# Moving one transposition and two product groups in the first block of a TensorE-bound kernel

## The chip, the cores and the metric

The kernel runs on one core of a Trainium2 chip. The metric is device time in microseconds (us) of that core; lower is better. Before the change the median of the first three runs was 1027.58 us. All runs compared here are of the fast state. The granted clock is the share of its full clock at which TensorE was allowed to run; where it differs between runs, the text says so, because that turned out to be the point.

## The reference

Retention (attention with a decay in place of a softmax) for 8 batches of 8 heads and 576 positions, then a two-layer block on 4608 tokens.

```python
scores = scale * q @ k.T                       # 8 x 8 heads, 576 x 576, head size 64
ret = scores * gamma ** (i - j)  (i >= j)      # masked decay
x = (ret @ v) laid out as (4608, 512)
h = x @ w_in                                   # 512 -> 2048
g = h * erf(softplus(h))
out = g @ w_out                                # 2048 -> 512
```

## The kernel before

Tokens come in 36 pieces of 128. Each piece has three stages: `transposes` (queries and keys through TensorE, copied by ScalarE out of PSUM, where this kernel has TensorE write its results), `scores` (TensorE, then a mask on VectorE) and `outputs` (TensorE, then scaling on VectorE; it also carries a state on to the next piece). Four pieces make one chunk of the two-layer block. The stages of later pieces are threaded between the products of earlier chunks, to keep TensorE at work (99% of the span). On ScalarE the trace shows the order in which the program is written: group 13's copy starts at 52.33, behind two rounding operations written ahead of it (51.17 and 51.75).

The first chunk's products come in sixteen groups, four for each quarter of the inner dimension; groups of a quarter need the rounded weights of that quarter. Each of the last four groups ends with a copy on ScalarE. Softplus and erf each begin with a table load on ScalarE (1.28 us each in this trace).

```python
def plain(self):                               # one yield = one group
    ...
    for dc in range(n_dc):                     # four quarters
        for n in range(4):
            for j in range(GP):
                nc.tensor.matmul(acc[n][...], lhsT=wa[...dc...], rhs=t[:, dc, ...])
            if dc == n_dc - 1:
                nc.scalar.copy(out=(self.t2 if tok else self.t1)[:, f], in_=acc[n])
            yield

def transposes(i):
    ...                                        # TensorE into PSUM, then on ScalarE:
    nc.scalar.copy(out=tT, in_=pt)

def rounding():                                # five steps for each part of the weights
    nc.scalar.activation(a_f, high_f, AF.Abs); nc.scalar.mul(...)   # step 1, ScalarE
    ...                                        # steps 2 to 5, VectorE (later parts end on GpSimd)
```

The order of the start is a string: `a` is the next stage of the next piece, `p` the next group, `w` a load of weights, a digit so many steps of rounding, `s` the store of the first chunk's input. Behind it come the softplus and the erf of the first chunk, the eighth piece's outputs, and the second chunk's groups with the ninth piece's stages.

```python
for what in "alkakakawkakakawaa3awwa2aaa5ppappawwppa5ppapp5wawcppa5ppappaa5s":
    ...
firsts[0].softplus()                           # table load, two activations on ScalarE
firsts[0].erf()                                # table load, two activations on ScalarE
most[0] = before_chunk(3)
attend(after_chunk(1))                         # eighth outputs
store_x(1)
for step, _ in enumerate(firsts[1].plain()):
    if step % 2 == 0:
        attend(min(done[0] + 1, most[0]))      # ninth transposition, ninth scores, ...
    round_weights(int(step > 1))
    ...
```

## Time and profile before

| | before |
|---|---|
| median of six runs, three of them taken with the changed kernel | 1027.55 us |
| span of the profiled run | 1026.0 us |
| TensorE busy | 1017.5 us (99%) |
| TensorE's listed waits, 42 to 66 us | 0.8 us ahead of the eighth outputs, 0.7 us ahead of group 9 |
| ScalarE busy | 390.4 us (38%) |

TensorE is the engine that sets the end (89% of the chain that ended last). A row of the view in order of time reads: start in us, length in us, engine, line of the kernel, operation, tile written and tiles read, shapes, count, and in brackets the idle time ahead of it with what ended it. The prediction shows the rows that matter.

### The profile page before, as it was taken

To read this page: it belongs to the slowest core of one execution; us is meant where nothing else is said; L and a number is where in the kernel's file an instruction comes from. 1 tells how busy PE (TensorE), PEld (TensorE's weight loads), DVE (VectorE), ACT (ScalarE), POOL (GpSimd) and SP (SyncE) were. 2 spreads that over 40 slices of the span, in tenths; PEclk is the share of its full clock that TensorE was granted. 3 is DMA by queue.
4 is the path that set the end of the run, shared out by engine and by line. 5 is a ranking of instruction groups with operands and counts; after the bars stand their busy time and mean duration, and the time that the engine had idled before them with its cause. 6 is when DMAs were issued, how large, how long until landed. Compare 5 with 4: busy or idle time off the path is not lost.

```text
span 1026.0 us, 15946 instructions
## 1 busy us (share of the span) xinstructions
PE 1017.5 (99%) x6346; PEld 876.1 (85%) x6346; DVE 669.1 (65%) x1054; ACT 390.4 (38%) x481; POOL 123.7 (12%) x122
## 2 busy tenths in 40 slices
PE   9999999999999999999999999999999999999998
PEld 8778888888888888888888888888888888888887
DVE  3868777877976656656666666666567655555555
ACT  2254134233234444434343444444433333333332
POOL 2143112122312110010001001000100000000000
PEclk9999999999999999999999999999999999999999
DMA  9999889979984344544444345444333334444333
GB/s 197 191 241 194 224 194 221 251 155 248 242 187 161 120 150 145 168 158 163 156 150 163 123 146 160 167 144 144 144 124 124 123 131 126 131 136 133 124 91 115
DMA packets 146986, 165.76 MB, mean 162 GB/s; under 512 B 97376, under 2 KB 121568, under 8 KB 138848
## 3 DMA queue, kind: packets, MB, share of 16 engines
q1 hardware_dynamic: 145904, 163.96, 56.5%
q8 instruction: 50, 0.82, 0.3%
q10 hardware_dynamic: 1008, 0.79, 0.3%
q14 instruction: 24, 0.20, 0.1%
HBM read 117.52 MB, written 47.19 MB: 161 GB/s over the span
## 4 chain that ended last, share of the span: by engine, by line
PE 89%; DMA 5%; DVE 3%; SPq 3%; issue 1%; POOL 0%; DVEq 0%; POOLq 0%
PE a L600 23%; PE a L492 22%; PE g L600 11%; PE g L492 11%; PE e L600 6%; PE e L492 5%; PE s L343 3%; PE o L361 2%; DMA raw_qs<-in_q_dram 1%; PE p L546 1%; SPq L145 1%; PE o L384 1%; PE o L372 1%; DMA raw_k<-in_k_dram 1%; SPq L131 1%; DMA raw_ks<-in_k_dram 1%
## 5 line engine op out<-in xcount | busy, mean ns | idle before, releaser
L492 PE MATMUL a<-x,wa 128*128 128x256 f32 x1088 | 258.3, 380 | 0.0
L492 PEld LDWEIGHTS a<-x,wa 128*128 128x128 f32 x1088 | 205.7, 190 | 28.5
L600 PE MATMUL a<-wb,s 128*128 128x256 f32 x864 | 205.7, 381 | 0.0
L600 PEld LDWEIGHTS a<-wb,s 128*128 128x128 f32 x864 | 162.9, 190 | 23.6 <-ACT o L614 0.7
L99 DVE TENSOR_TENSOR t<-g,t 128x512 f32<-128x512 f32 x68 | 46.9, 690 | 150.3 <-ACT t L522 113.1
L492 PE MATMUL g<-x,wa 128*128 128x256 f32 x544 | 129.2, 380 | 0.0
L492 PEld LDWEIGHTS g<-x,wa 128*128 128x128 f32 x544 | 102.8, 190 | 14.4
L99 DVE TENSOR_TENSOR o<-a,o 128x512 f32<-128x512 f32 x108 | 74.2, 687 | 49.3 <-PE a L600 49.3
L517 ACT COPY t<-a 128x512 f32<-128x512 f32 x34 | 19.9, 586 | 188.2 <-PE a L492 188.2
L99 DVE TENSOR_TENSOR t<-t,s 128x1024 f32<-128x1024 f32 x72 | 89.6, 1285 | 0.0
L561 ACT ACTIVATE s<-t 128x1024 f32<-128x1024 f32 x72 | 72.1, 1049 | 27.8 <-DVE t L99 27.8
L270 POOL TENSOR_TENSOR wraw<-wraw 128x512 f32<-128x512 f32 x28 | 29.5, 1053 | 435.6 <-DVE wraw L268 178.9
L99 DVE TENSOR_TENSOR x<-x 128x512 f32<-128x512 f32 x115 | 75.8, 692 | 1.2
L528 ACT COPY t<-a 128x512 f32<-128x512 f32 x34 | 19.9, 587 | 144.4 <-PE a L492 144.4
L565 ACT ACTIVATE s<-s 128x1024 f32<-128x1024 f32 x72 | 72.1, 1049 | 0.4
L600 PE MATMUL g<-wb,s 128*128 128x256 f32 x288 | 68.6, 381 | 0.0
L600 PE MATMUL e<-wb,t 128*128 128x256 f32 x288 | 68.5, 380 | 0.0
L600 PE MATMUL a<-wb,t 128*128 128x256 f32 x288 | 68.5, 380 | 0.0
L600 PE MATMUL g<-wb,t 128*128 128x256 f32 x288 | 68.2, 380 | 0.0
L99 DVE TENSOR_TENSOR sT<-s,cst 128x512 f32<-128x512 f32 x72 | 46.2, 682 | 32.5 <-PE s L343 32.5
L99 DVE TENSOR_TENSOR o<-g,o 128x512 f32<-128x512 f32 x72 | 49.3, 684 | 24.6 <-ACT o L614 19.8
L492 PE MATMUL e<-x,wa 128*128 128x256 f32 x272 | 64.8, 381 | 0.0
(75 smaller groups left out, 1226.2 us busy)
## 6 DMA issues: line engine op xcount, KB each, us to landing
od<-o SPq DMA_DIRECT2D x54, 512.0 KB, 3.3
x<-xd SPq DMA_DIRECT2D x27, 1024.0 KB, 4.8
o<-od SPq DMA_DIRECT2D x27, 1024.0 KB, 5.2
raw_qs<-in_q_dram SPq DMA_DIRECT2D x96, 112.0 KB, 4.4
raw_ks<-in_k_dram SPq DMA_DIRECT2D x84, 112.0 KB, 4.1
xd<-x SPq DMA_DIRECT2D x9, 1024.0 KB, 5.3
raw_k<-in_k_dram SPq DMA_DIRECT2D x64, 128.0 KB, 4.5
raw_v<-in_v_dram SPq DMA_DIRECT2D x64, 128.0 KB, 4.5
```

Source lines behind the costliest of these rows:

```text
L99: nc.vector.tensor_tensor(out=out, in0=in0, in1=in1, op=op)
L131: nc.sync.dma_start(out=t[part * SQ : (part + 1) * SQ, :, at : at + m - SQ], in_=tokens[:, :, d0 : d0 + m - SQ])
L145: nc.sync.dma_start(out=t[r0 : r0 + n, e::2, :], in_=heads.rearrange("h p d -> p h d"))
L270: engine.tensor_tensor(out=r_f, in0=high_f, in1=r_f, op=ALU.mult)
L343: nc.tensor.matmul(ps[e][:, p, :], lhsT=t["kT"][heads[e], p, :], rhs=t["qT"][heads[e], p, :], start=True, stop=True)
L361: nc.tensor.matmul(o[p % 2][heads[(e + p) % 2], p // 2, :], lhsT=t["v"][:, 2 * p + e, :], rhs=t["sT"][:, e, p, :], start=(p < 2), stop=(no ...
L492: nc.tensor.matmul(acc[:, j * TH : (j + 1) * TH], lhsT=weights["wa", self.g][:, a, d, j * P : (j + 1) * P], rhs=x[self.g, self.c][a][:, d, :],
L517: nc.scalar.copy(out=self.t1[:, 1], in_=self.a)
L528: nc.scalar.copy(out=self.t2[:, 0], in_=self.a)
L561: nc.scalar.activation(self.s[:, j], t, AF.Softplus)
L565: nc.scalar.activation(self.s[:, j], self.s[:, j], AF.Erf)
L600: nc.tensor.matmul(acc[:, tp, :], lhsT=left[:, j * TH + tp * P : j * TH + (tp + 1) * P], rhs=weights["wb", self.g][:, b, j, :], start=(sta ...
```

## The change

It is meant to fill TensorE's two waits in the first chunk: the seventh piece's transposition (and the load of weights `w` behind it) goes ahead of the third quarter (groups 9 and 10), which waits for its weights, and groups 15 and 16 go behind the eighth scores, so that they run while VectorE masks those scores and the eighth outputs find their mask ready.

```diff
-    for what in "alkakakawkakakawaa3awwa2aaa5ppappawwppa5ppapp5wawcppa5ppappaa5s":
+    for what in "alkakakawkakakawaa3awwa2aaa5ppappawwppa5ppawapp5wcppa5ppaaapp5s":
```

## The prediction

> **What bounds the kernel now.** I read four views in this order: the page, the totals of TensorE's waits, TensorE in order of time from 43 to 65 us, and ScalarE over the same stretch. First the page.
>
> ```profile
> span 1026.0 us, 15946 instructions
> PE 1017.5 (99%) x6346; PEld 876.1 (85%) x6346; DVE 669.1 (65%) x1054; ACT 390.4 (38%) x481; POOL 123.7 (12%) x122
> PEclk9999999999999999999999999999999999999999
> PE 89%; DMA 5%; DVE 3%; SPq 3%; issue 1%; POOL 0%; DVEq 0%; POOLq 0%
> ```
>
> TensorE is busy 1017.5 of 1026.0 us at full clock and carries 89% of the chain that ended last. So only its 8.5 idle us can be saved, while a new TensorE wait lengthens the run by its full size, because almost nothing later can absorb it: after 64 us one wait is listed, of 0.2 us (last line here). The first three lines are the totals of the waits from 42 to 66 us.
>
> ```profile
> PE o L361 <- POOL state L423: 0.8, 1, 0.8
> PE p L546 <- DVE wa L271: 0.7, 1, 0.7
> PEld o L361 <- DVE sT L99: 0.4, 1, 0.4
> ...
> PE s L343 <- DVE kT L322: 0.2, 1, 0.2
> ```
>
> The change aims at these waits. I number pieces and groups from one: group 1 to 16 are the first block's products (L546, two to a row of x8), piece 7's transposition is the first pt_q row below, pt_k with it. TensorE in order of time (start, length):
>
> ```profile
> 44.40 1.99 PE L546 MATMUL p<-x,wa 128*128 128x256 f32 x8 [0.72 <-DVE wa L271]
> 46.23 0.60 PE L328 MATMUL pt_q<-ident,raw_q 128*128 128x128 f32 x4
> ...
> 50.02 1.99 PE L546 MATMUL p<-x,wa 128*128 128x256 f32 x8
> ...
> 52.72 1.03 PE L546 MATMUL pe<-x,wa 128*128 128x256 f32 x4
> 53.59 1.03 PE L546 MATMUL pg<-x,wa 128*128 128x256 f32 x4
> 54.54 1.09 PE L361 MATMUL o<-sT,raw_v 128*64 128x128 f32 x16
> 56.78 1.16 PE L343 MATMUL s<-qT,kT 64*128 64x128 f32 x16
> 58.76 1.64 PE L361 MATMUL o<-sT,raw_v 128*64 128x128 f32 x16 [0.82 <-POOL state L423]
> ```
>
> The third quarter (groups 9 to 12) starts at 44.40 after waiting 0.72 us for its rounded weights. Groups 15 and 16 (pe, pg) run before the seventh outputs and the eighth scores (56.78); those scores are followed straight by the eighth outputs, which need their mask from VectorE first. The wait is put down to GpSimd's state, but only 2 of the 16 products run before 59.31, when the second mask has ended (59.26): scores end at 57.94, outputs could have gone on at once, so about 1.3 us are lost there.
>
> ScalarE, same stretch:
>
> ```profile
> 53.75 0.60 ACT L334 COPY kT<-pt_k 128x512 f32<-128x512 f32 x1
> 54.23 0.61 ACT L555 COPY t<-pe 128x512 f32<-128x512 f32 x1
> 54.70 0.62 ACT L555 COPY t<-pg 128x512 f32<-128x512 f32 x1
> 55.18 0.73 ACT L250 ACTIVATE wb<-wraw 128x512 f32<-128x512 f32 x1
> 55.76 0.72 ACT L251 ACTIVATE wraw<-wraw 128x512 f32<-128x512 uint32 x1
> 56.50 1.28 ACT L561 ACT_TABLE_LOAD   x1
> 57.79 2.00 ACT L561 ACTIVATE s<-t 128x1024 f32<-128x1024 f32 x2
> 59.81 1.28 ACT L565 ACT_TABLE_LOAD   x1
> 61.11 2.01 ACT L565 ACTIVATE s<-s 128x1024 f32<-128x1024 f32 x2
> 63.15 0.59 ACT L334 COPY kT<-pt_k 128x512 f32<-128x512 f32 x1
> ```
>
> This is what I build on: from the copy of group 16 (54.70) to the copy of the ninth piece's keys (63.15) ScalarE has no gap. That copy ends at 63.74, and the ninth scores, which need it, run at 64.77. The chain has about one microsecond of slack.
>
> [...] group 13's copy starts at 52.33, behind two rounding operations (51.17, 51.75), though its products were through about a microsecond earlier. [...] The trace has 1283 ns for each of two loads here, but the softplus starts 0.01 us behind its load[...]. [...] L255 and L259 take 0.79 and 1.15 us beside GpSimd work at 45.15 to 46.96, against 0.43 when alone.
>
> **The change, part by part.** No instruction is added or removed; the order of loads on the queue, of weight roundings and of PSUM buffers stays. Two stretches of TensorE's order move.
>
> Part one, transposition ahead of group 9. It takes 47.10 - 46.23 = 0.87 us and the idle time before group 9 is 0.72 us, so it fills the wait: group 9 would start at about 43.68 + 0.87 = 44.55 instead of 44.40, and groups 9 to 12 and the seventh scores end at about 49.3 instead of 50.02. Its data is there: the piece's last key load is issued at 36.09 and lands 8.0 us later, 44.1, just when those products are due. But group 13 needs the fourth weight part, whose last step on VectorE ends at 49.94; in the kernel before this is hidden to within 0.1 us. It cannot come earlier, and now comes a little later: its two ScalarE steps, done at 42.25 to 43.54 before, are queued behind the two transposition copies (about 44.4 to 45.5), so VectorE's L255 can start at about 46.1 instead of 45.26; it then waits for GpSimd's value weighting (45.73 plus 1.04 gives 46.8) and ends at about 47.05. L259 to L271 follow with 0.45, 0.72, 0.43+0.1, 0.72, 0.69 between starts and ends: 50.2. So group 13 starts at 50.25, 0.2 later than before. Part one earns nothing: -0.7 turns into +0.2.
>
> Part two, groups 15 and 16 behind the eighth scores. From 50.25: groups 13 and 14 and the eighth transposition 2.70 (52.72 - 50.02), seventh outputs 2.24 (56.78 - 54.54), eighth scores 1.10, groups 15 and 16 1.82 plus 0.1: through at about 58.2. Masks of the eighth scores end at about 57.7, hidden beside those groups. The eighth outputs run from 58.2 to 60.4 instead of ending at 61.54: +0.2 - 1.3 = -1.1 us. This is the intended gain.
>
> The price is on ScalarE. Group 16's copy now waits for group 16: later by seventh outputs and eighth scores, 54.54 to 57.88 = 3.34, plus 0.1, plus the 0.2 above = 3.64 us. All behind it is in order and without a gap, so it moves whole: softplus, erf, and the ninth piece's key copy, which ends at 63.74 + 3.64 = 67.38. TensorE, 1.1 us early, reaches the ninth scores at 64.77 - 1.1 = 63.6 and stands until 67.45. Scores move from 64.77 to 67.45, +2.7 us. Everything behind is TensorE-bound; one small gap ahead of the tenth piece's transposition (67.70 to 67.98, from the same rows) should close, -0.2. Net +2.5 us: 1027.6 + 2.5 = 1030.1.
>
> **Rivals.** (a) The gains stand and the ScalarE chain hides: -1.1 us, or -1.9 if the fourth weight part also came early; 1025.7 to 1026.5. For it: ScalarE is busy only 38% overall. Against: its order puts the ninth keys' copy behind the erf, and those 10 lines have no gap. (b) The stall of 3.8 us at the ninth scores also throttles TensorE. [...] No gap after the start in the trace before is long enough to test it. (c) A load becomes late because the transposition triggers the ninth piece's query load. The queue reaches that load at 54.98 only, long after its trigger, and its order is kept; I give it nothing, at most a few tenths through the 44.1 landing, which the slack ahead of group 13 swallows. (d) Later phases absorb the shift: only 0.2 us of listed waits lie behind 64 us, so 1029.9 at the lowest.
>
> **Range and chances.** Centre 1030.1, with 0.2 for the throttling tail and run spread: 1030.2. Three runs before spread by 1.2 us. Errors of the chain sum are about half a microsecond on either side, so 1028.8 to 1032.0. All rivals stay within 0.5% of the time, far from 2%: same 0.98.
>
> **What would show it.** Part one: the wait of 0.72 us for L271 ahead of group 9 gone, and one of near a microsecond ahead of group 13 in its place, again for L271. Part two: eighth outputs without a wait; group 16's copy near 58.3; a TensorE wait of 3.5 to 4 us at the ninth scores, ended by the key copy on ScalarE; busy time of TensorE unchanged, idle time up. Wrong if the ninth scores start before 65 us, if the key copy runs ahead of the erf, or if TensorE waits for a load in 60 to 70 us.

## The result and the profile after

The changed kernel took 1032.68 us (median of 6 runs, 1030.36 to 1033.56) against 1027.55 us (6 runs). The ratio is 1.0048, with a 95% interval of 1.0035 to 1.0060. Ratios here are the mean time of one kernel's fast runs over that of the other's of the same rounds, so not quite the ratio of the medians. The sign and the place of the loss were as predicted; the size was not: 5.1 us where 2.6 were forecast, and above the stated range.

The page of the changed kernel (same parts as in the prediction: span, busy time, chain that ended last):

```profile
span 1030.6 us, 15945 instructions
PE 1018.5 (99%) x6346; PEld 877.0 (85%) x6346; DVE 666.8 (65%) x1054; ACT 390.2 (38%) x481; POOL 122.4 (12%) x122
PE 95%; DVE 1%; ACT 1%; SPq 1%; DMA 1%; issue 0%; POOL 0%; POOLq 0%; ACTq 0%; DVEq 0%
```

TensorE's busy time grew by 1.0 us though it does the same work, and its idle time by 3.6 us. TensorE's waits of the changed kernel from 42 to 75 us (total, count, longest):

```profile
PE s L343 <- ACT kT L334: 3.4, 1, 3.4
PE p L546 <- DVE wa L271: 1.1, 1, 1.1
```

Both waits of before are gone from their places. The one for L271 now stands ahead of group 13 and has grown, as the prediction said, and a new one of 3.4 us is ended by ScalarE's copy of the ninth keys. TensorE in order of time:

```profile
50.68 1.99 PE L546 MATMUL p<-x,wa 128*128 128x256 f32 x8 [1.09 <-DVE wa L271]
...
57.77 1.03 PE L546 MATMUL pg<-x,wa 128*128 128x256 f32 x4
58.73 1.09 PE L361 MATMUL o<-sT,raw_v 128*64 128x128 f32 x16
...
63.24 1.10 PE L546 MATMUL pe<-x,wa 128*128 128x256 f32 x4
67.73 1.60 PE L343 MATMUL s<-qT,kT 64*128 64x128 f32 x16 [3.39 <-ACT kT L334]
69.25 2.07 PE L546 MATMUL pg<-x,wa 128*128 128x256 f32 x4
```

The eighth outputs (58.73) follow group 16 without a wait: that half of the intent works. The ninth scores then stand until 67.73. The last row is the surprise: the same four instructions that took 1.13 us before take 2.07 us. The same two rows in the kernel before:

```profile
64.77 1.16 PE L343 MATMUL s<-qT,kT 64*128 64x128 f32 x16
65.86 1.13 PE L546 MATMUL pg<-x,wa 128*128 128x256 f32 x4
```

ScalarE in order of time shows who held the scores:

```profile
53.68 0.59 ACT L334 COPY kT<-pt_k 128x512 f32<-128x512 f32 x1
57.97 0.58 ACT L555 COPY t<-pe 128x512 f32<-128x512 f32 x1 [3.70 <-PE pe L546]
58.84 0.59 ACT L555 COPY t<-pg 128x512 f32<-128x512 f32 x1 [0.28 <-PE pg L546]
...
65.20 2.00 ACT L565 ACTIVATE s<-s 128x1024 f32<-128x1024 f32 x2
67.11 0.56 ACT L334 COPY kT<-pt_k 128x512 f32<-128x512 f32 x1
```

It stood 3.70 us waiting for group 15, did the softplus and the erf that much later, and copied the ninth keys last. Stretches of the changed kernel, with busy us and number of instructions of TensorE, its weight loads, VectorE, ScalarE and GpSimd, their granted clock of TensorE, and the DMA's share and GB/s:

```profile
66.00:68.00 2.00, 0.27 (x4) 0.27 (x6) 0.00 (x0) 2.00 (x4) 1.26 (x2) 1.00 0.97 406
68.00:70.00 2.00, 2.00 (x18) 1.69 (x17) 0.65 (x2) 0.80 (x2) 0.00 (x0) 0.57 1.21 262
70.00:72.00 2.00, 2.00 (x7) 1.61 (x6) 2.00 (x6) 0.00 (x0) 0.00 (x0) 0.57 1.16 377
```

After the stall the clock was 0.57 in two stretches of 2 us. The trace's clock record has 0.5 for 3.413 us, from 68.3 us on, and 1.0 on both sides. A window, here and below, is a stretch of that length.

The difference of the two spans, 1030.57 - 1025.96 = 4.61 us, adds up from landmarks in the two traces. To the end of the third weight part (44.34 and 44.68): +0.34, ahead of the change. From there to group 13 (5.68 and 6.00): +0.32. To the ninth scores (14.75 and 17.05): +2.30. To the ninth outputs (5.50 and 6.81): +1.31. The same stretch takes 5.19 us where the clock stays full (e1_fill below), so this is 1.6 us of lowered clock, less the 0.3 us gap ahead of the tenth transposition, which closed. From there to the end (955.69 and 956.03): +0.34, of which a wait at a later piece's scores, 0.2 before and 0.6 after, is the most.

### The profile page after: what moved, and what is told of

Read it like the earlier page. It is cut to its first block, busy times and chain, and to the rows that moved or that the text cites. A ratio compares the mean times of both kernels' runs of the same rounds, so it can differ in the third digit from the quotient of the medians.

```text
span 1030.6 us, 15945 instructions
## 1 busy us (share of the span) xinstructions
PE 1018.5 (99%) x6346; PEld 877.0 (85%) x6346; DVE 666.8 (65%) x1054; ACT 390.2 (38%) x481; POOL 122.4 (12%) x122
## 4 chain that ended last, share of the span: by engine, by line
PE 95%; DVE 1%; ACT 1%; SPq 1%; DMA 1%; issue 0%; POOL 0%; POOLq 0%; ACTq 0%; DVEq 0%
PE a L600 24%; PE a L492 23%; PE g L600 12%; PE g L492 12%; PE e L600 6%; PE e L492 6%; PE s L343 3%; PE o L361 3%; PE o L384 2%; PE o L372 1%; PE p L546 1%; PE pg L546 1%; SPq L145 1%; DMA wraw<-in_moe_w_in_dram 1%; PE pe L546 1%; PE idle L706 0%
```

## The experiments

Theory: ScalarE's order moves the ninth keys' copy behind the late softplus and erf, TensorE stalls for it (3.4 us), and the stall brings a window at half clock, as the changed kernel's trace has it (0.5 for 3.413 us). All experiments ran on one chip (that of the first result is not on record), with the kernel before in the same rounds; there its medians were 1028.33, 1028.10 and 1028.53 us, and single runs spread over 3 to 4 us, so ratios and the recorded clock of each run count for more than a median. I call a run lowered when its mean clock is 0.998 or less; all 102 runs of the kernel before in these rounds have 0.999 or 1.000.

**The stall filled (e1_fill).** The changed kernel, with products of no use in the idle stretch, into a PSUM bank that is overwritten next.

```diff
+                    if (self.c, dc, n) == (1, 0, 2):
+                        for _ in range(12):
+                            nc.tensor.matmul(acc[3][:, :P], lhsT=ident, rhs=ident, start=True, stop=True)
```

> The changed kernel with 12 identity products (some 3.2 us of TensorE work of no use) put just ahead of the ninth scores, into the idle stretch. Theory (the stall lets the clock be halved for one window of 3.413 us, worth 1.7 us): the ninth scores still start near 67.7, but the granted clock is 1.0 after it, every run lies near 1030.4, as the one unthrottled run of the changed kernel (1030.36). Rival (the extra 2 us come from something else behind the stall, loads or VectorE): still 1032 to 1033.5.

Measured: 1030.28 us (10 runs), ratio 1.0019 (1.0009 to 1.0028); no run lowered. TensorE in order of time:

```profile
67.42 1.16 PE L343 MATMUL s<-qT,kT 64*128 64x128 f32 x16 [0.69 <-ACT kT L334]
68.52 1.13 PE L546 MATMUL pg<-x,wa 128*128 128x256 f32 x4
```

The scores start as late as in the changed kernel and the next group again takes 1.13 us, at a mean clock of 0.999. Work that does nothing made the kernel faster: the mean is 1030.43 us, against 1032.18 for e3_part_two (below), which has the stall unfilled in the same rounds. So the clock's share of the loss is shown. Two of the ten runs reached 1031.4 and 1032.2 us at full clock; on this chip that is within the spread that the kernel before has too.

**Part one alone (e2_part_one).** The load `w` moves with the transposition, as in the change.

```diff
-    ..."ppa5ppapp5wawcppa5ppappaa5s"
+    ..."ppa5ppawapp5wcppa5ppappaa5s"
```

> Only the transposition ahead of group 9. Theory: the wait of 0.7 us moves to group 13, where the fourth weight part comes 0.2 to 0.4 us later than before; 1027.6 to 1028.0, no stall above 1.5 us, no lowered clock. Rival (the part's gain is real and hidden in the changed kernel by the other): 1026.8.

Measured: 1028.02 us (13 runs), ratio 0.9999 (0.9991 to 1.0007), none lowered. Group 13 waits 1.1 us for L271 and starts 5.99 us after the third weight part (44.50 to 50.49), against 5.68 before. The part moves the wait and earns nothing that these runs can see.

**Part two alone (e3_part_two).**

```diff
-    ..."ppa5ppappaa5s"
+    ..."ppa5ppaaapp5s"
```

> Only groups 15 and 16 behind the eighth scores. Theory: the whole loss is here: ninth scores about 67.3, stall 3.4 to 3.8 us, most runs 1031.5 to 1033 with one window at half clock, a rare one near 1030. Rival (both parts are needed for the loss): within 0.5 us of the kernel before.

Measured: 1032.29 us (5 runs), ratio 1.0039 (1.0026 to 1.0052), all five lowered. The stall is 3.4 us again, and the ninth scores come 22.73 us after the third weight part (44.75 to 67.48), against 20.43 before and 23.05 in the changed kernel: +2.30 of part two and +0.32 of part one make up the whole. The loss is part two's.

**The erf behind the ninth transposition (e4_erf_later).** The changed kernel with one call moved.

```diff
     firsts[0].softplus()
-    firsts[0].erf()
...
             attend(min(done[0] + 1, most[0]))
+        if step == 0:
+            firsts[0].erf()
```

> The changed kernel with the erf emitted after the ninth piece's transposition, so that its key copy is not behind the erf's table load and two activations (3.3 us). Theory (ScalarE's order is the cause): key copy near 64.0, stall at the ninth scores 0.5 to 1.0 us, clock 1.0, 1027.0 to 1027.6, at or a little under the kernel before. Rival (the key copy is late for another reason, or PSUM or VectorE hold the ninth scores): stays above 1029.5.

Measured: 1027.50 us (21 runs), ratio 0.9993 (0.9986 to 0.9999), none lowered. The copy runs at 63.80, before the erf, and the scores follow almost without a gap:

```profile
64.42 1.16 PE L343 MATMUL s<-qT,kT 64*128 64x128 f32 x16
```

One move on ScalarE takes the whole loss away and leaves a gain of about 0.7 us by the ratio (interval 0.1 to 1.4): the cause is the order on ScalarE.

**The changed kernel again (e7_after_again), unaltered.**

> The changed kernel unaltered, to have it on the same chip and in the same rounds as the next three. Theory: stall of 3.4 us at the ninth scores, most runs with a mean clock of 0.996 to 0.998 and 3.5 to 5.5 us over the kernel before; a run with clock 0.999 or 1.000, if there is one, only 1.5 to 3 us over it. Rival (the lowered clock was chance in the first six runs[...]): most runs at 0.999 or 1.000 and about 2.5 us over the kernel before.

Measured: 1032.21 us (5 runs), ratio 1.0038 (1.0024 to 1.0052), all five lowered. The rival of chance falls: with the first six runs and part two alone, 15 of 16 runs with this stall were lowered. Its profile shows a second form of the loss. The clock record has 0.5 for 6.827 us, two windows, from 67.0 us on. TensorE in order of time:

```profile
68.02 2.08 PE L343 MATMUL s<-qT,kT 64*128 64x128 f32 x16 [3.38 <-ACT kT L334]
70.03 2.07 PE L546 MATMUL pg<-x,wa 128*128 128x256 f32 x4
71.89 1.91 PE L546 MATMUL p<-x,wa 128*128 128x256 f32 x4
```

Here the clock was lowered while TensorE still stood, so the scores run slow too. The window from 67.0 to 70.4 had 1.0 us of standing and 2.4 us of work, and the clock was still 0.50 from 70.5 to 73.0; it was 1.00 from 74.0 on.

**Shorter stalls (e8_fill_half, e5_half_erf, e10_fill_nine).** The filled kernel with 6 and with 9 identity products, and the changed kernel with only the second half of the erf moved.

```diff
-                        for _ in range(12):
+                        for _ in range(6):     # e8;  e10: range(9)
```

```diff
-    firsts[0].erf()
+    firsts[0].erf((0,))
...
+        if step == 0:
+            firsts[0].erf((1,))
```

The expectation of e8_fill_half names two outcomes, one after the other: no lowered run at all, or some.

> The filled kernel with 6 identity products in place of 12 (some 1.4 us of work), so about 2.0 us of TensorE stay idle, while the ninth scores start at the same time. [...] never lowered, 2.5 us over the kernel before. [...] lowered in some of the runs (mean clock 0.998 or less), those about 4.5 us over it.

Measured: 1031.48 us (7 runs), ratio 1.0029 (1.0018 to 1.0040). The second outcome came: four of seven lowered (mean clock 0.997 or 0.998); these average 1031.91 us, the other three 1030.68. So a lowered clock cost 1.2 us here, not the 2 us that the expectation gave it. TensorE stood 2.0 us in the profiled run, which kept its full clock.

> The changed kernel with only the second half of the erf (1.0 us) emitted after the ninth piece's transposition. Theory: the key copy is 1.0 us earlier, stall 2.4 us, time without a lowered clock 1.0 us under that of the changed kernel, so some 1.5 us over the kernel before; with 2.4 us idle the clock is lowered in a part of the runs, which then lie 3.2 us over. Rival (ScalarE's order is not what holds the scores): like the changed kernel.

Measured: 1030.59 us (14 runs), ratio 1.0024 (1.0016 to 1.0032). Nine of fourteen lowered, average 1031.33 us, the other five 1029.83. TensorE in order of time:

```profile
67.22 1.16 PE L343 MATMUL s<-qT,kT 64*128 64x128 f32 x16 [2.44 <-ACT kT L334]
```

> The filled kernel with 9 identity products: about 1.3 us of TensorE stay idle at the ninth scores, which start at the same time. From the shares of lowered runs so far (0 of 10 with 0.7 us idle, 4 of 7 with 2.0, 9 of 14 with 2.4, 15 of 16 with 3.4) [...] no run here is lowered (mean clock 0.999 or 1.000 in all), 2 to 2.5 us over the kernel before. If the chance just grows with the idle time: about a third of the runs lowered.

Measured: 1030.58 us (8 runs), ratio 1.0024 (1.0013 to 1.0034). None lowered, with a stall of 1.4 us. So with stalls of 2.0 and 2.4 us, shorter than the window of 3.413 us, the clock was lowered in part of the runs (e8_fill_half, e5_half_erf); with 1.4 and 0.7 us it was in none of 8 and 10 runs of the filled kernel.

**A version to beat both, first try (e6_best).**

```diff
-    ..."wwppa5ppawapp5wcppa5ppaaapp5s"        # the changed kernel
+    ..."wwppa5ppa1wapp4wcppaa5ppaaqpp1s"      # q: first half of the softplus
...
-    firsts[0].softplus()
-    firsts[0].erf()
+    firsts[0].softplus((1,))
...
+        if step == 0:
+            firsts[0].erf()
+            round_weights(4)
```

> A version meant to beat both: eighth transposition ahead of groups 13 and 14, fourth part's ScalarE steps ahead of the seventh transposition's copies, first half of the softplus ahead of groups 15 and 16, erf and the last rounding steps behind the ninth transposition. Theory: no TensorE wait over 0.4 us between 44 and 70 us, 2 us under the kernel before (0.9 for group 13's wait filled, 1.1 to 1.3 for the eighth outputs'), clock 1.0. Rival (a new wait of VectorE or GpSimd takes the place): within 1 us of the kernel before.

Measured: 1027.60 us (21 runs), ratio 0.9994 (0.9987 to 1.0000): the rival was right. ScalarE in order of time shows one reason:

```profile
58.90 1.28 ACT L250 ACT_TABLE_LOAD   x1
60.20 0.68 ACT L250 ACTIVATE wb<-wraw 128x512 f32<-128x512 f32 x1
...
61.47 1.28 ACT L562 ACT_TABLE_LOAD   x1
```

The rounding's absolute value (L250), put between the two halves of the softplus, brought two table loads of 1.28 us with it (the same operation behind the erf, at 67.52, brought none; why is not shown), and the ninth scores waited 0.6 us. Group 13 still waited 0.5 us: VectorE's L268 took 1.15 us, from 48.28 on, where it overlapped GpSimd's weighting of values (48.07 to 49.15) that I had moved forward; alone it took 0.43. One of the 21 runs (1028.75 us, clock 0.998) counts as lowered; it has no trace, and the profiled run, with waits of 0.6 and 0.5 us, kept its full clock, so why is not shown.

**Second try (e9_best2).**

```diff
-    ..."ppa1wapp4wcppaa5ppaaqpp1s"
+    ..."ppa1wapp4wcppa5app1aaqpps"
```

> The version meant to beat both, mended: the fifth step of rounding no longer lies between the two halves of the softplus (it cost two more table loads), and the eighth transposition comes behind the first rounding of the second weights, so that the weighting of values does not hold up VectorE's L268 (1.15 in place of 0.43 us). Theory: no wait over 0.3 us at the ninth scores or ahead of group 13, two table loads again in place of four before the ninth scores' end, 1.5 to 2.2 us under the kernel before. Rival: again only 0.5 us under it.

Measured: 1026.76 us (22 runs), ratio 0.9987 (0.9978 to 0.9996): faster than the kernel before by 0.13%, and the lowest ratio of all, though inside the 2% that count as the same. The two table loads are gone (with only the copies of groups 15 and 16, at 56.71 and 57.57, between the two halves of the softplus, no load comes between them), and so is the long L268 (0.43 us again). TensorE's waits from 42 to 80 us are down to one:

```profile
PE pt_k L328 <- DMA raw_k<-in_k_dram: 2.1, 1, 2.1
```

Now the load of the tenth piece's keys is late in the profiled run. Two of the 22 runs were lowered (1030.56 and 1033.05 us); that this wait was what lowered them fits its length (2.1 us; with 2.0 us four of the seven runs of e8_fill_half were lowered) but is not shown, since neither has a trace. The profiled run (1028.80 us) is 2.0 us above the median, so most runs may not have the wait at all. The gain of 1.5 to 2.2 us in the expectation is met by the medians (1.8 us), but by the ratio it is 1.3 us, with an interval of 0.4 to 2.3.

## Why the prediction was wrong

**What held.** Part one: the wait moved to group 13, which came 0.32 us later where 0.2 was worked out; part one alone showed the same 0.31. VectorE's L255 took 1.00 us (46.38 to 47.38) beside GpSimd's weighting (46.06 to 47.10), where about 47.05 was named for its end. Part two: the eighth outputs lost their wait; group 16's copy came at 58.84, or 58.5 without the 0.34 us by which this run was late before the change, against 58.3; the stall at the ninth scores is there, 3.4 us against "3.5 to 4". The scores came 2.62 us later, counted from the third weight part, against 2.7. The small gap ahead of the tenth transposition closed. The cause, ScalarE's order, is shown by moving one call. Rival (a) is refuted by the changed kernel, (c) by the absence of load waits between 60 and 75 us, and (d) is right that almost nothing absorbs the shift. One sign did not come: TensorE's busy time was to stay unchanged and grew by 1.0 us, which fits the lowered clock.

**What failed.** The step that failed is the weighing of rival (b). Its sum carried 0.2 us for the clock, on an estimate that a stall of 3.8 us would seldom lower it, which no trace had shown. Measured, 15 of 16 runs with a stall of 3.4 us were lowered. The cost, by an estimate from the clock records, is half of the work time in them: 1.7 us for the 3.413 us at 0.5 of the changed kernel's trace, 2.9 us for e7_after_again (6.827 us less the 1.0 us of standing in them, half of 5.8 us). With the term at these sizes the sum is 1031.8 to 1033.0, and the median of 1032.68 lies between. Only one of the first six runs has a trace; for the others their mean clocks allow an estimate. Half of 3.413 us is 0.0017 of a run of 1030 us, half of 6.827 us is 0.0033; the profiled run of the changed kernel, with the first, has 0.998, that of e7_after_again, with the second, 0.996, and the 102 runs of the kernel before have 0.999 or 1.000. So 0.996 fits two windows (1033.56 and 1032.95 us) and 0.998 one (1032.35 and 1032.41); 0.997 (1033.50) can be either. The one full-clock run of the six took 1030.36 us, 0.2 above the centre of the prediction: without the lowered clock its sum was right.

**Why the estimate was wrong.** It rested on no trace. In the changed kernel's trace the lowered clock starts at 68.3, and in the 3.413 us before that, from 64.9 on, TensorE worked from 67.73 on, 0.6 of the 3.4 us. The trace of the kernel before could have warned: its last products end at 1021.8, and the clock is 1.00 to 1024.5 and 0.50 from 1024.51 on, 2.7 us behind them. The prediction looked for a long gap inside the kernel and missed the one behind its end.

By runs, the clock was lowered in 15 of 16 with a stall of 3.4 us, in 9 of 14 with 2.4 us and in 4 of 7 with 2.0 us, and in none of 8 with 1.4 us and of 10 with 0.7 us. These are few runs, the stalls are those of the profiled run of each kernel, and the ends of products are modelled. What lies between 1.4 and 2.0 us, and why some runs with the same stall were lowered and others not, is not shown.

The length of the lowered clock differed too: 3.413 us in the changed kernel's trace, where TensorE worked throughout (3.41 of 3.41 us from 68.3 on), and 6.827 us in e7_after_again, where it stood for the first 1.0 us. That the standing made the difference is not shown by two traces.

## What to carry to other kernels

When a change delays an engine that is idle most of the time, follow that engine's queue to its next consumer: a copy that the bound engine needs may stand behind long work that nobody is waiting for, and moving that work behind the copy costs one line. A TensorE stall can cost more than its length: here stalls of 2.0, 2.4 and 3.4 us came with a lowered clock in 4 of 7, 9 of 14 and 15 of 16 runs, and that cost 1.2 to 2.9 us on top, by estimates from those runs; stalls of 1.4 and 0.7 us came with none in 8 and 10 runs. The recorded mean clock of each run, not only of the profiled one, shows whether that happened.
